# Gate taps of chunk 2 split over three engines in the last eight blocks, and a longer first loop

## The chip, the core and the metric

The kernel runs on one core of a Trainium2 chip. The metric is the device time of one launch in microseconds. A core has TensorE (PE, matrix products into PSUM), VectorE (DVE), ScalarE (ACT), GpSimd (POOL), and SyncE (SP), which here only issues DMAs. Each engine works through its own instructions in the order in which the program records them, and waits on semaphores for the others.

## The reference

A causal convolution over time with softmax weights per head, then a gated projection. For 8 sequences of 4224 tokens and 192 channels:

```python
w = exp(weight - weight.max(-1)); w = w / (w.sum(-1) + 1e-9)      # 8 heads, 7 taps
x2 = einsum('hk,bskhg->bshg', w, x_unf)                           # 7-tap causal convolution
gate_pre = sum(conv_w[k] * xp[:, k:k+S, :] for k in range(5))     # 5-tap causal convolution per channel
gate = 1 / (1 + exp(-gate_pre))
out = (gate * (x2 @ w_val)) @ w_out                               # 192 x 192 each
```

`xp` is the first convolution's output with four zero rows ahead of it.

## The kernel before, in words

**Layout.** The eight sequences are two streams of four sequences each, laid end to end. The 192 channels are split in two chunks. Chunk 1 is 128 channels on 128 partitions, with the two streams side by side (tile x1, so a block of m tokens is 128 x 2m). Chunk 2 is the other 64 channels, with the two streams stacked on 128 partitions (tile x2, a block is 128 x m). The tokens are cut into 14 groups, and these into 36 blocks, numbered 0 to 35: blocks 0 and 1 of about 303 tokens, 2 to 7 of 448, 8 to 31 of 502, 32 and 33 of 448, 34 of 500 and 35 of 188.

**The first convolution.** It is done by PE in units of four windows (`conv_unit`, L312), against a banded matrix. ACT copies each unit from PSUM to a tile e (L321), and DMAs from SP's queue spread the rows of e into x1 and x2 of a group (L350). A table `todo` says how many units are recorded in which block's pass: 3 in passes 0, 2, 6 and 7, five in passes 3 and 4, four in pass 5, 3, 3 and 4 in turn in the middle, 2 in passes 26 to 31, and none after.

**One block n.** The steps are functions that the loops call with a block's number.

- *The gate* is five taps per chunk. `gate_open(n, i)` (L384) is the first tap: ACT multiplies x by a column of weights into PSUM (pa for chunk 1, i = 0; pb for chunk 2, i = 1; one bank set each, so pa is opened for the next block only after it is closed). `gate_taps` (L391) is the other four: DVE instructions of the form x * weight + acc, in place in PSUM. `gate_close` (L404) is ACT's sigmoid into a tile g (g1 for chunk 1, g2 for chunk 2).
- *The split* (`split`, L412 and L420 on ACT, L413 and L421 on POOL): ACT rounds x to a short float xh, POOL subtracts to get the rest xl. The products with w_val are then made as wh xh + wl xh + wh xl.
- *The value product* v = x w_val is in three PSUM banks: bank 2 (`diagonal`, L447, then `columns`, L485) and banks 0 and 1 (`main`, L457, then `rows`, L470).
- `gated` (L504): DVE multiplies a bank of v by g in place. This is the last reader of that bank, so it also sets it free.
- `split_gated1` and `split_gated2`: the same split on g, ACT's ph and POOL's pl.
- *The output product* o = g w_out: the same four steps with ph and pl, one block later. `project` (L520) copies o to SBUF by ACT and issues the output DMA.

**Banks.** One pool of five PSUM banks ("p") serves v, o and the convolution units. A new tile takes the bank that was set free longest ago. The second bank of o in `rows("o", n-1)` takes the one that v's bank 2 of the same pass had, so it waits for `gated(n, 2)`.

**The order around the change.** The scheduler is off (`manual_schedule`): each engine runs what the two loops at the end record, in that order. A pass n of a loop makes v for block n, o for block n-1, and the gate of block n+1, and opens the gates of block n+2. The two loops differ in where DVE's and ACT's work stands. The first loop (passes 0 to HEAD-1, with HEAD = 4) records two chunk-1 taps of block n+1 ahead of `gated(n, ...)`, and the other two and the four chunk-2 taps behind it, and ACT closes pa of block n+1 late, among the convolution copies. The second loop (from pass HEAD on) records all four chunk-1 taps ahead of `gated(n, 2)`, closes and opens pa right after them, and records the four chunk-2 taps behind `gated(n, 1)`. `split(n+1)` stands in the front part of both.

Of the kernel before, what the change touches and what calls it, by code (L numbers as in the profile page):

```python
# [7 lines left out]
F32 = mybir.dt.float32  # L8
# [4 lines left out]
ALU = mybir.AluOpType  # L13
# [29 lines left out]
def second(n):  # L43
    return NS * n * WIN - reach(n)
# [24 lines left out]
STEPS = []  # L69
# [5 lines left out]
N = len(STEPS)  # L75
LAST = N - 1
MB = 502
# [24 lines left out]
def kernel(  # L102
# [9 lines left out]
    nc = tc.nc  # L112
# [6 lines left out]
    pp = ctx.enter_context(tc.tile_pool(name="pp", bufs=2))  # L119
    op = ctx.enter_context(tc.tile_pool(name="op", bufs=3))  # L120
# [54 lines left out]
    def scratch(n, i):  # L175
        o = scr_at[i]
        scr_at[i] += n
        return scr[i][:, o : o + n].bitcast(I32)

    raw = {}  # L180
    for name, ap, n, i in (("wv", wv, 2 * D + 2 * KG, 2), ("wo", wo, 2 * D, 1)):
        t = scratch(2 * n, i)
# [74 lines left out]
    cwt = cp.tile([128, 2, KG], F32, name="cwt")  # L257
# [107 lines left out]
    def views(n, k=KG - 1):  # L365
        g, o, m = STEPS[n]
        b = second(NJS[g])
        x1v = x1s[g][:, : 2 * b].rearrange("p (a t) -> p a t", a=2)
        return x1v[:, :, o + k : o + k + m], x2s[g][:, o + k : o + k + m]
# [5 lines left out]
    def gate_open(n, i):  # L375
        if n >= N:
            return
        m = STEPS[n][2]
        if i == 0:
            acc = ps_g.tile([128, 2, 512], F32, tag="pa", name=f"pa_{n}")[:, :, :m]  # L380
        else:
            acc = ps_h.tile([128, 512], F32, tag="pb", name=f"pb_{n}")[:, :m]
        accs[n, i] = acc
        nc.scalar.mul(acc, views(n, 0)[i], cwt[:, i, 0:1])  # L384

    def gate_taps(n, i, k0=1, k1=KG):
        if n >= N:
            return
        acc = accs[n, i]
        for k in range(k0, k1):  # L390
            nc.vector.scalar_tensor_tensor(  # L391
                out=acc, in0=views(n, k)[i], scalar=cwt[:, i, k : k + 1],
                in1=acc, op0=ALU.mult, op1=ALU.add,
            )

    def gate_close(n, i):
        if n >= N:
            return
        m = STEPS[n][2]
        if i == 0:  # L400
            dst = g1s[n] = gp.tile([128, 2, MB], F32, tag="g1", name=f"g1_{n}")[:, :, :m]
        else:
            dst = g2s[n] = gp.tile([128, MB], F32, tag="g2", name=f"g2_{n}")[:, :m]
        nc.scalar.activation(dst, accs.pop((n, i)), AF.Sigmoid)  # L404
# [3 lines left out]
    def split1(pool, tag, n, x):  # L408
        m = STEPS[n][2]
        h = pool.tile([128, 2, MB], F32R, tag="h", name=f"{tag}h_{n}")[:, :, :m]  # L410
        l = pool.tile([128, 2, MB], F32R, tag="l", name=f"{tag}l_{n}")[:, :, :m]
        nc.scalar.copy(h, x)  # L412
        nc.gpsimd.tensor_tensor(out=l, in0=x, in1=h.bitcast(F32), op=ALU.subtract)  # L413
        return h, l

    def split2(pool, tag, n, x):
        m = STEPS[n][2]
        h = pool.tile([128, MB], F32R, tag="h2", name=f"{tag}h2_{n}")[:, :m]
        l = pool.tile([128, MB], F32R, tag="l2", name=f"{tag}l2_{n}")[:, :m]
        nc.scalar.copy(h, x)  # L420
        nc.gpsimd.tensor_tensor(out=l, in0=x, in1=h.bitcast(F32), op=ALU.subtract)  # L421
        return h, l
# [3 lines left out]
    def bank(what, n, q):  # L426
        t = ps.tile([128, 512], F32, tag="p", name=f"{what}_{n}_{q}")[:, : STEPS[n][2]]
        banks[what, n, q] = t
        return t

    def operands(what, n):
        return (w_val, *xs[n, 1], *xs[n, 2]) if what == "v" else (w_out, *pr[n, 1], *pr[n, 2])

    def parts(w, h, l):
        return (w.h, h), (w.l, h), (w.h, l)

    def ok(n):
        return 0 <= n < N

    def diagonal(what, n):  # L440
        if not ok(n):
            return
        acc = bank(what, n, 2)
        w, _, _, h2, l2 = operands(what, n)
        r = slice(W22, W22 + 128)
        for i, (a, b) in enumerate(parts(w, h2, l2)):
            nc.tensor.matmul(acc, lhsT=a[:, r], rhs=b, start=(i == 0), stop=False)  # L447

    def main(what, n, q):
        if not ok(n):  # L450
            return
        fresh = (what, n, q) not in banks
        acc = bank(what, n, q) if fresh else banks[what, n, q]
        w, h, l, _, _ = operands(what, n)
        r = slice(W11, W11 + 128)
        for i, (a, b) in enumerate(parts(w, h, l)):
            nc.tensor.matmul(  # L457
                acc, lhsT=a[:, r], rhs=b[:, q], start=(fresh and i == 0), stop=(not fresh and i == 2)
            )

    def rows(what, n):
        if not ok(n):
            return
        fresh = (what, n, 0) not in banks
        two = [bank(what, n, q) if fresh else banks[what, n, q] for q in range(2)]
        w, _, _, h2, l2 = operands(what, n)
        r = slice(W21, W21 + 128)
        for i, (a, b) in enumerate(parts(w, h2, l2)):
            for acc, p in zip(two, HALVES):
                nc.tensor.matmul(  # L470
                    acc, lhsT=a[p, r], rhs=b[p], start=(fresh and i == 0), stop=(not fresh and i == 2)
                )

    def columns(what, n):
        if not ok(n):
            return
        m = STEPS[n][2]
        acc = banks[what, n, 2]
        w = w_val if what == "v" else w_out
        x = views(n)[0] if what == "v" else g1s[n]  # L480
        cuts = [m * i // 4 for i in range(5)]
        for i in range(4):
            c = slice(cuts[i], cuts[i + 1])
            for q, p in enumerate(HALVES):
                nc.tensor.matmul(  # L485
                    acc[p, c], lhsT=w.f[:, W12 : W12 + 64], rhs=x[:, q, c],
                    start=False, stop=(i == 3),
                )

    def split(n):  # L490
        if n >= N:
            return
        x1, x2 = views(n)
        if n == 0:
            xs[n, 2] = split2(sp, "x", n, x2)
        xs[n, 1] = split1(sp, "x", n, x1)
        if n > 0:
            xs[n, 2] = split2(sp, "x", n, x2)

    def gated(n, q):  # L500
        if not ok(n):
            return
        v = g1s[n][:, q] if q < 2 else g2s[n]
        nc.vector.tensor_tensor(out=v, in0=banks.pop(("v", n, q)), in1=v, op=ALU.mult)  # L504

    def split_gated1(n):
        if ok(n):
            pr[n, 1] = split1(pp, "p", n, g1s[n])

    def split_gated2(n):  # L510
        if ok(n):
            pr[n, 2] = split2(pp, "p", n, g2s[n])

    def project(n, q):
        if not ok(n):
            return
        m = STEPS[n][2]
        if n not in ots:
            ots[n] = op.tile([128, 3 * MB], F32, tag="ot", name=f"ot_{n}")
        nc.scalar.copy(ots[n][:, q * m : (q + 1) * m], banks.pop(("o", n, q)))  # L520
        o = 3 * sum(s[2] for s in STEPS[:n])
        if n == LAST:
            nc.sync.dma_start(out[:, o + q * m : o + (q + 1) * m], ots[n][:, q * m : (q + 1) * m])
        elif q == 1:
            nc.sync.dma_start(out[:, o : o + 3 * m], ots[n][:, : 3 * m])
# [34 lines left out]
    split(0)  # L560
    w_out.join(nc.gpsimd)
    gate_taps(0, 0)
    conv(first_unit[LAG] - done[0])
    gate_close(0, 0)
    gate_open(1, 0)
    w_out.cast(nc.gpsimd)
    gate_taps(0, 1)
    gate_close(0, 1)
    gate_open(1, 1)

    for n in range(HEAD):
        k = 2 if n < 2 else 3
# [150 lines left out]
```

## Time and profile before

| | |
|---|---|
| median of 3 runs | 390.23 us (390.02 to 390.97) |
| the profiled execution's own time | 393.35 us |
| its span in the profile | 391.6 us |
| granted TensorE clock, mean | 0.991 |
| busy share: PE, DVE, ACT, POOL | 97%, 87%, 83%, 65% |
| HBM traffic over the span | 141 GB/s |

Times in the profile's rows are microseconds from the span's start. A row of the timeline has a start, a time that it covers, the engine, the line of the code, the operation, output and inputs (buffer numbers left out), the shape and a count, and in brackets the engine's idle time ahead of it and what ended that. A row with a count above 1 is a run of equal instructions, and its second number covers the run. PE's matrix products are pipelined: the distance of two starts is what one takes from the engine. The profiled execution is 3.1 us longer than the median of the timed runs; differences are worked out against it.

### The profile page before, as it was taken

How to read it: one execution, taken by the hardware profiler on the slowest of the kernel's cores; microseconds unless marked ns; L12 is line 12 of the kernel's file. 1: busy time of each engine (PE TensorE's matmuls, PEld its weight loads, DVE VectorE, ACT ScalarE, POOL GpSimd, SP SyncE). 2: the span in 40 equal slices, each digit the busy share in tenths (PEclk: the TensorE clock that was granted, in tenths of full speed). 3: DMA queues.
4: the chain of work that ended last, by engine and by line, in shares of the span. 5: the costliest groups of instructions: out<-in, count | busy, mean ns of one | idle time of the engine just before them, and what ended most of it. 6: DMA issues, size and time to landing. Idle time of an engine off the chain costs nothing.

```text
span 391.6 us, 8620 instructions
## 1 busy us (share of the span) xinstructions
PE 378.0 (97%) x3204; PEld 321.6 (82%) x3204; DVE 342.3 (87%) x424; ACT 323.8 (83%) x525; POOL 254.8 (65%) x177
## 2 busy tenths in 40 slices
PE   8699999999999999999999999999999999999895
PEld 8687988898888888888888888888888787788684
DVE  4669899888998998998999899899899999999970
ACT  7458888988888888888889988888888888887863
POOL 1959765566667665666665666766566676776871
PEclk9969999999999999999999999999999999999999
DMA  8777869998687689778868868758987644333223
GB/s 293 210 195 223 253 214 290 258 239 272 210 251 216 180 260 256 210 217 253 224 194 256 219 185 261 218 178 253 257 226 227 211 160 146 114 135 133 80 106 144
DMA packets 38209, 82.49 MB, mean 211 GB/s; under 512 B 4856, under 2 KB 17528, under 8 KB 38168
## 3 DMA queue, kind: packets, MB, share of 16 engines
q1 hardware_dynamic: 36720, 79.90, 67.6%
q0 software_dynamic: 896, 1.31, 1.4%
q10 hardware_dynamic: 552, 0.73, 0.6%
q8 instruction: 25, 0.41, 0.5%
q14 instruction: 16, 0.13, 0.1%
HBM read 29.34 MB, written 26.00 MB: 141 GB/s over the span
## 4 chain that ended last, share of the span: by engine, by line
PE 72%; DVE 13%; DMA 5%; ACT 4%; issue 3%; SPq 2%; POOL 0%; DVEq 0%; ACTq 0%
PE pc L312 20%; PE o L457 10%; PE v L457 9%; PE v L485 7%; PE v L470 6%; PE o L485 6%; DVE pa L391 6%; PE o L470 5%; PE o L447 5%; PE v L447 4%; DVE pb L391 4%; DVE g L504 3%; DMA x<-e 2%; DMA x<-xw 2%; DMA scr<-wv 1%
## 5 line engine op out<-in xcount | busy, mean ns | idle before, releaser
L391 DVE SCALAR_TENSOR_TENSOR pa<-x,cwt,pa 128x1004 f32<-128x1004 f32 (+5 forms) x144 | 172.9, 1201 | 10.7 <-ACT pa L384 6.8
L413 POOL TENSOR_TENSOR xl<-x,xh 128x1004 fp32r<-128x1004 f32 (+5 forms) x36 | 74.8, 2077 | 73.1 <-ACT xh L412 58.9
L312 PEld LDWEIGHTS pc<-band,x 128*120 128x120 f32 x912 | 103.1, 187 | 7.1 <-issue 3.9
L312 PE MATMUL pc<-band,x 128*120 128x122 f32 x912 | 104.2, 272 | 4.3 <-DMA x<-xw 3.8
L391 DVE SCALAR_TENSOR_TENSOR pb<-x,cwt,pb 128x502 f32<-128x502 f32 (+5 forms) x144 | 102.2, 710 | 3.8
L413 POOL TENSOR_TENSOR pl<-g,ph 128x1004 fp32r<-128x1004 f32 (+5 forms) x36 | 79.4, 2204 | 10.3 <-ACT ph L412 7.7
L504 DVE TENSOR_TENSOR g<-v,g 128x502 f32<-128x502 f32 (+5 forms) x108 | 65.8, 642 | 21.1 <-PE v L470 16.1
L404 ACT ACTIVATE g<-pa 128x1004 f32<-128x1004 f32 (+5 forms) x36 | 34.5, 959 | 38.8 <-DVE pa L391 21.1
L321 ACT COPY e<-pc 120x488 f32<-120x488 f32 x114 | 59.1, 586 | 6.4 <-PE pc L312 6.3
L421 POOL TENSOR_TENSOR pl<-g,ph 128x502 fp32r<-128x502 f32 (+5 forms) x36 | 43.0, 1194 | 32.8 <-ACT ph L420 32.7
L520 ACT COPY ot<-o 128x502 f32<-128x502 f32 (+5 forms) x108 | 56.2, 551 | 3.3 <-PE o L457 2.6
L421 POOL TENSOR_TENSOR xl<-x,xh 128x502 fp32r<-128x502 f32 (+5 forms) x36 | 41.8, 1162 | 0.0
L384 ACT ACTIVATE pa<-x,cwt 128x1004 f32<-128x1004 f32 (+5 forms) x36 | 37.8, 1051 | 4.8 <-DMA x<-e 3.7
L485 PEld LDWEIGHTS v<-x,wvf 128*64 128x64 f32 x576 | 29.1, 136 | 11.8 <-issue 11.4
L485 PE MATMUL v<-x,wvf 128*64 128x125 f32 (+4 forms) x576 | 37.2, 270 | 0.0
L412 ACT CAST ph<-g 128x1004 fp32r<-128x1004 f32 (+5 forms) x36 | 35.1, 976 | 1.5 <-DVE g L504 1.5
L485 PE MATMUL o<-g,wof 128*64 128x125 f32 (+4 forms) x576 | 35.6, 264 | 0.0
L412 ACT CAST xh<-x 128x1004 fp32r<-128x1004 f32 (+5 forms) x36 | 34.6, 961 | 0.0
L485 PEld LDWEIGHTS o<-g,wof 128*64 128x64 f32 x576 | 30.9, 136 | 0.1
L457 PE MATMUL o<-ph,woh 128*128 128x502 f32 (+5 forms) x72 | 30.9, 429 | 0.0
L457 PE MATMUL v<-xh,wvh 128*128 128x502 f32 (+5 forms) x72 | 27.2, 377 | 0.3 <-ACT e L321 0.3
L457 PE MATMUL v<-xh,wvl 128*128 128x502 f32 (+5 forms) x72 | 27.1, 377 | 0.0
(75 smaller groups left out, 573.1 us busy)
## 6 DMA issues: line engine op xcount, KB each, us to landing
x<-xw SPq DMA_DIRECT2D x64, 300.0 KB
out<-ot SPq DMA_DIRECT2D x24, 753.0 KB
x<-e SPq DMA_DIRECT2D x40, 285.9 KB
x<-xw SPq DMA_DIRECT2D x20, 360.0 KB
out<-ot SPq DMA_DIRECT2D x8, 672.0 KB
x<-e SPq DMA_DIRECT2D x32, 141.6 KB
x<-e SPq DMA_DIRECT2D x25, 171.6 KB
x<-e SPq DMA_DIRECT2D x16, 94.4 KB
```

The costliest lines, as they stand in the source:

```text
L312: nc.tensor.matmul(pc[:M, k * WIN : (k + 1) * WIN], lhsT=xtiles[i][:, c : c + M], rhs=band[:, 4 * q + hi, :], start=True, stop=True,)
L321: nc.scalar.copy(e[:, a : a + w], pc[:M, :w])
L384: nc.scalar.mul(acc, views(n, 0)[i], cwt[:, i, 0:1])
L391: nc.vector.scalar_tensor_tensor(out=acc, in0=views(n, k)[i], scalar=cwt[:, i, k : k + 1], in1=acc, op0=ALU.mult, op1=ALU.add,)
L412: nc.scalar.copy(h, x)
L413: nc.gpsimd.tensor_tensor(out=l, in0=x, in1=h.bitcast(F32), op=ALU.subtract)
L421: nc.gpsimd.tensor_tensor(out=l, in0=x, in1=h.bitcast(F32), op=ALU.subtract)
L457: nc.tensor.matmul(acc, lhsT=a[:, r], rhs=b[:, q], start=(fresh and i == 0), stop=(not fresh and i == 2))
L470: nc.tensor.matmul(acc, lhsT=a[p, r], rhs=b[p], start=(fresh and i == 0), stop=(not fresh and i == 2))
L485: nc.tensor.matmul(acc[p, c], lhsT=w.f[:, W12 : W12 + 64], rhs=x[:, q, c], start=False, stop=(i == 3),)
L504: nc.vector.tensor_tensor(out=v, in0=banks.pop(("v", n, q)), in1=v, op=ALU.mult)
L520: nc.scalar.copy(ots[n][:, q * m : (q + 1) * m], banks.pop(("o", n, q)))
```

## The change

Two edits.

1. HEAD is 6 instead of 4, so that passes 4 and 5 run in the first loop's order.
2. A new step, `aside(n)`, for the blocks 28 to 35, recorded in the second loop behind `split(n+1)`. ACT multiplies the view of tap 3 of chunk 2 by its weight into a new tile t. The view of tap 4 is multiplied into a new tile u, by POOL for blocks 28 to 32, and by ACT for blocks 33 to 35. POOL adds u to t. For these blocks `gate_taps` does only taps 1 and 2 of chunk 2, and then DVE adds t to the accumulator pb.

```diff
-HEAD = 4
+HEAD = 6
+ASIDE, BOTH = 28, 33
...
+    asides = {}
+
+    def aside(n):
+        if not ASIDE <= n < N:
+            return
+        m = STEPS[n][2]
+        t = asides[n] = pp.tile([128, MB], F32, tag="t", name=f"t_{n}")[:, :m]
+        u = pp.tile([128, MB], F32, tag="u", name=f"u_{n}")[:, :m]
+        nc.scalar.mul(t, views(n, 3)[1], cwt[:, 1, 3:4])
+        if n < BOTH:
+            nc.gpsimd.tensor_scalar(
+                out=u, in0=views(n, 4)[1], scalar1=cwt[:, 1, 4:5], scalar2=None, op0=ALU.mult
+            )
+        else:
+            nc.scalar.mul(u, views(n, 4)[1], cwt[:, 1, 4:5])
+        nc.gpsimd.tensor_tensor(out=t, in0=t, in1=u, op=ALU.add)
...
     def gate_taps(n, i, k0=1, k1=KG):
...
+        if i == 1 and n in asides:
+            k1 = 3
         for k in range(k0, k1):
...
+        if i == 1 and n in asides:
+            nc.vector.tensor_tensor(out=acc, in0=asides.pop(n), in1=acc, op=ALU.add)
...
         split(n + 1)
+        aside(n + 1)
         diagonal("o", n - 1)
```

What it moves, engine by engine. VectorE in passes 4 to 6, before; pa and pb are the gate accumulators with the block's number behind them, g2 and g1 the outputs of `gated`:

```order
L391 SCALAR_TENSOR_TENSOR pa_5_819<-x1_2_387,cwt_155,pa_5_819 128x2x448 x4
L504 TENSOR_TENSOR g2_4_854<-v_4_2_858,g2_4_854 128x448
L504 TENSOR_TENSOR g1_4_817<-v_4_0_876,g1_4_817 128x448
L504 TENSOR_TENSOR g1_4_817<-v_4_1_880,g1_4_817 128x448
L391 SCALAR_TENSOR_TENSOR pb_5_856<-x2_2_388,cwt_155,pb_5_856 128x448 x4
L391 SCALAR_TENSOR_TENSOR pa_6_897<-x1_3_555,cwt_155,pa_6_897 128x2x448 x4
L504 TENSOR_TENSOR g2_5_989<-v_5_2_993,g2_5_989 128x448
L504 TENSOR_TENSOR g1_5_895<-v_5_0_1011,g1_5_895 128x448
L504 TENSOR_TENSOR g1_5_895<-v_5_1_1015,g1_5_895 128x448
L391 SCALAR_TENSOR_TENSOR pb_6_991<-x2_3_556,cwt_155,pb_6_991 128x448 x4
L391 SCALAR_TENSOR_TENSOR pa_7_1032<-x1_3_555,cwt_155,pa_7_1032 128x2x448 x4
L504 TENSOR_TENSOR g2_6_1122<-v_6_2_1126,g2_6_1122 128x448
```

The same engine from pass 5's first taps on in the changed kernel (its line numbers are 22 to 24 higher):

```order
L413 SCALAR_TENSOR_TENSOR pa_6_956<-x1_3_555,cwt_155,pa_6_956 128x2x448 x2
L528 TENSOR_TENSOR g2_5_989<-v_5_2_993,g2_5_989 128x448
L528 TENSOR_TENSOR g1_5_954<-v_5_0_1009,g1_5_954 128x448
L528 TENSOR_TENSOR g1_5_954<-v_5_1_1013,g1_5_954 128x448
L413 SCALAR_TENSOR_TENSOR pa_6_956<-x1_3_555,cwt_155,pa_6_956 128x2x448 x2
L413 SCALAR_TENSOR_TENSOR pb_6_991<-x2_3_556,cwt_155,pb_6_991 128x448 x4
L413 SCALAR_TENSOR_TENSOR pa_7_1094<-x1_3_555,cwt_155,pa_7_1094 128x2x448 x4
L528 TENSOR_TENSOR g2_6_1122<-v_6_2_1126,g2_6_1122 128x448
```

Two of the four chunk-1 taps have moved behind the three `gated` instructions in passes 4 and 5. The first pass with all four ahead of them is now pass 6.

GpSimd in pass 29 of the changed kernel; xl and xl2 are the rests of x for the next block, pl2 and pl those of g:

```order
L437 TENSOR_TENSOR xl_30_3924<-x1_11_3295,xh_30_3923 128x1004
L445 TENSOR_TENSOR xl2_30_3928<-x2_11_3296,xh2_30_3927 128x502
L399 TENSOR_SCALAR u_30_3932<-x2_11_3296,cwt_155 128x502
L404 TENSOR_TENSOR t_30_3931<-t_30_3931,u_30_3932 128x502
L445 TENSOR_TENSOR pl2_29_3972<-g2_29_3913,ph2_29_3971 128x502
L437 TENSOR_TENSOR pl_29_3994<-g1_29_3848,ph_29_3993 128x1004
```

Two instructions have come in between xl2 and pl2; before, these four stood one behind the other without them. VectorE at the end of pass 28 and in pass 29 of the changed kernel:

```order
L413 SCALAR_TENSOR_TENSOR pb_29_3804<-x2_11_3296,cwt_155,pb_29_3804 128x502 x2
L418 TENSOR_TENSOR pb_29_3804<-t_29_3820,pb_29_3804 128x502
L413 SCALAR_TENSOR_TENSOR pa_30_3850<-x1_11_3295,cwt_155,pa_30_3850 128x2x502 x4
L528 TENSOR_TENSOR g2_29_3913<-v_29_2_3917,g2_29_3913 128x502
L528 TENSOR_TENSOR g1_29_3848<-v_29_0_3940,g1_29_3848 128x502
L528 TENSOR_TENSOR g1_29_3848<-v_29_1_3944,g1_29_3848 128x502
```

Where four pb taps stood in a row, two are left, and the add that reads t stands between them and the next block's pa taps.

## The prediction

> **What bounds the kernel now.** I read the page first (PE is busy for 97% of the span, DVE for 87%), then the busy times by windows, then the timelines of PE, VectorE (DVE), ScalarE (ACT) and GpSimd (POOL) at three places: passes 3 to 7, passes 27 to 31, and pass 34. "Pass n" is the run of the loop for block n, and Tn is where its first product starts (L447, v from xh and wvh). A window late in the kernel (PE, PE's weight loads, DVE, ACT, POOL, then PE's granted clock and the DMA share):
>
> ```profile
> 331.00:341.00 10.00, 10.00 (x80) 8.03 (x82) 9.77 (x12) 8.74 (x14) 6.84 (x5) 1.00 0.33 112
> ```
>
> PE is full, and its clock is granted in full. But a PE that counts as busy can be one that is held, and DVE is full as well here (9.77 of 10). How much PE is held shows in the length of its passes, so I measure everything by these. Early, with the PE rows that open passes 4 to 8, the convolution units of passes 3 and 5, and the one product that waits:
>
> ```profile
> 58.85 4.36 PE L312 MATMUL pc<-band,x 128*120 128x122 f32 x40
> 62.98 0.45 PE L447 MATMUL v<-xh,wvh 128*128 128x448 f32 x1
> 68.97 0.47 PE L470 MATMUL o<-ph,woh 64*128 64x448 f32 x1 [0.59 <-DVE g L504]
> 75.24 0.45 PE L447 MATMUL v<-xh,wvh 128*128 128x448 f32 x1
> 82.30 3.52 PE L312 MATMUL pc<-band,x 128*120 128x122 f32 x32
> 85.58 0.45 PE L447 MATMUL v<-xh,wvh 128*128 128x448 f32 x1
> 95.08 0.45 PE L447 MATMUL v<-xh,wvh 128*128 128x448 f32 x1
> 105.06 0.47 PE L447 MATMUL v<-xh,wvh 128*128 128x502 f32 x1
> ```
>
> One unit costs 4.36 - 3.52 = 0.84 us. Pass 6, with three units, lasts 9.50; pass 5, with four, 10.34, just one unit more. So neither is held. Pass 4 with five should last 11.18 and lasts 12.26: it loses 1.08, at the product that waits for `gated` to free v's bank 2. Pass 7, three units, lasts 9.98 and loses 0.48.
>
> **Edit 1: the first order in passes 4 and 5.** DVE and ACT there:
>
> ```profile
> 62.62 1.01 ACT L384 ACTIVATE pa<-x,cwt 128x896 f32<-128x896 f32 x1
> ...
> 60.40 2.86 DVE L391 SCALAR_TENSOR_TENSOR pb<-x,cwt,pb 128x448 f32<-128x448 f32 x4
> 63.66 4.73 DVE L391 SCALAR_TENSOR_TENSOR pa<-x,cwt,pa 128x896 f32<-128x896 f32 x4 [0.41 <-ACT pa L384]
> 68.30 1.68 DVE L504 TENSOR_TENSOR g<-v,g 128x448 f32<-128x448 f32 x3
> 78.99 0.63 DVE L504 TENSOR_TENSOR g<-v,g 128x448 f32<-128x448 f32 x1 [1.60 <-PE v L485]
> 80.55 1.16 DVE L504 TENSOR_TENSOR g<-v,g 128x448 f32<-128x448 f32 x2 [0.93 <-PE v L470]
> ```
>
> Before, pass 4 has `gated` at 68.30, T4 + 5.32, and loses 1.08; so a 448-token pass loses what `gated` starts later than T + 4.24. With two taps ahead of it instead of four (4.64 us, so 2.32 less) DVE is ready at T4 + 3.0 and waits for PE's columns, T + 3.75 as in pass 5. **Pass 4 loses nothing: -1.08.**
>
> The work put off comes back in pass 6, the first of the second loop. In pass 5 the two chunk-1 `gated` start at T5 + 5.31 and end near 6.4; then come two pa taps (2.32) and four pb taps (2.8): DVE is through at T5 + 11.5, and pass 5 is 10.34, so T6 + 1.1. ACT is later still. In pass 3, which has the first order, pa is open at 62.62 + 1.01, which is 4.78 after the units begin at 58.85. In pass 5 they begin at T5 + 7.06, so pa of block 7 opens at T5 + 11.84, T6 + 1.50. Four taps of 4.64 from T6 + 1.53 put `gated(6, 2)` at T6 + 6.17, 1.93 past the limit. **Pass 6 loses 1.93.** Pass 7 then starts at T6 + 11.43; DVE is done with block 6 and the pb taps at T6 + 6.17 + 1.6 + 2.8 = T6 + 10.6, and its pa taps (5.08, from 315.12 to 320.20 below) end at T7 + 4.25: **the 0.48 of pass 7 goes.** Sum: -1.08 + 1.93 - 0.48 = **+0.37**. If ACT opens pa in time, DVE alone sets T6 + 1.1 and the sum is -0.06; if pass 7 keeps its 0.48 it is +0.85. Behind it PE stays the bound up to pass 25, so this is carried to the end. SP's and POOL's queues keep their order here.
>
> **Edit 2: prices.** Per block DVE loses two taps of 0.745 (from 312.14 to 315.12 for four, below) and gains one add:
>
> ```profile
> L504 DVE TENSOR_TENSOR g<-v,g 128x502 f32<-128x502 f32 x72 | 46.5, 676 | 12.1 <-PE v L470 11.4 <-PE v L485 0.4
> L413 POOL TENSOR_TENSOR xl<-x,xh 128x1004 fp32r<-128x1004 f32 x24 | 51.6, 2150 | 53.6 <-ACT xh L412 45.5 <-DMA x<-e 4.3 <-issue 2.2
> L421 POOL TENSOR_TENSOR xl<-x,xh 128x502 fp32r<-128x502 f32 x24 | 29.1, 1211 | 0.0
> L269 POOL MEMSET wof<- 128x128 f32 x1 | 0.2, 206 | 0.0
> L701 POOL MEMSET const-float32-1.0<- 128x1 f32 x1 | 0.1, 99 | 0.0
> ```
>
> The add reads PSUM and SBUF as `gated` does: 676 ns, 0.63 from start to start. So DVE saves 0.86 a block if it does not wait. POOL's add of t is the 1.21 row. POOL's multiply u is nowhere in the trace. Its upper end is the two-operand row, 1.21. Its lower end is a memset, which reads nothing: (206 - 99)/127 = 0.84 ns an element, 0.52 us for 502. Two operands cost (2150 - 1211)/502 = 1.87 ns an element; one operand less at half of that gives 1.21 - 0.47 = 0.74, which I take, between the ends and nearer to the write-only one. The Trainium skill, GPSIMD Engine Reference, section 3.1, gives 1.8 cycles an element at 1.2 GHz for the best one-input loop of that length and about 2.6 for two inputs; by that u would be an estimated 0.75 us, and the sum would be the same.
>
> ACT's multiply by a weight (0.6 to 0.7 us, as its casts) falls in the gap in which ACT waits for DVE's pa taps, 1.19 in the row below, so it costs nothing; if that gap closes, it is 0.6 a block.
>
> **Edit 2: passes 28 to 31.** PE's passes, DVE, ACT and POOL:
>
> ```profile
> 315.07 0.47 PE L447 MATMUL v<-xh,wvh 128*128 128x502 f32 x1
> 324.89 0.47 PE L447 MATMUL v<-xh,wvh 128*128 128x502 f32 x1
> 334.85 0.47 PE L447 MATMUL v<-xh,wvh 128*128 128x502 f32 x1
> 344.67 0.48 PE L447 MATMUL v<-xh,wvh 128*128 128x502 f32 x1
> 354.18 0.45 PE L447 MATMUL v<-xh,wvh 128*128 128x448 f32 x1
> ...
> 312.14 3.08 DVE L391 SCALAR_TENSOR_TENSOR pb<-x,cwt,pb 128x502 f32<-128x502 f32 x4
> 315.12 5.17 DVE L391 SCALAR_TENSOR_TENSOR pa<-x,cwt,pa 128x1004 f32<-128x1004 f32 x4
> 320.20 1.97 DVE L504 TENSOR_TENSOR g<-v,g 128x502 f32<-128x502 f32 x3
> 350.54 1.27 DVE L504 TENSOR_TENSOR g<-v,g 128x502 f32<-128x502 f32 x2 [0.38 <-PE v L470]
> ...
> 320.41 1.01 ACT L404 ACTIVATE g<-pa 128x1004 f32<-128x1004 f32 x1 [1.19 <-DVE pa L391]
> ...
> 308.49 2.15 POOL L413 TENSOR_TENSOR xl<-x,xh 128x1004 fp32r<-128x1004 f32 x1 [1.69 <-ACT xh L412]
> 310.60 1.26 POOL L421 TENSOR_TENSOR xl<-x,xh 128x502 fp32r<-128x502 f32 x1
> 318.84 2.15 POOL L413 TENSOR_TENSOR xl<-x,xh 128x1004 fp32r<-128x1004 f32 x1 [1.68 <-DMA out<-ot]
> 324.63 2.36 POOL L413 TENSOR_TENSOR pl<-g,ph 128x1004 fp32r<-128x1004 f32 x1 [0.21 <-ACT ph L412]
> 328.68 2.16 POOL L413 TENSOR_TENSOR xl<-x,xh 128x1004 fp32r<-128x1004 f32 x1 [1.69 <-ACT xh L412]
> ```
>
> Pass 31 lasts 9.51 and is not held; passes 28, 29 and 30 last 9.82, 9.96 and 9.82. Pass 28 has `gated` at T + 5.13 and loses 0.31, so here the limit is T + 4.82. All there is to gain is 0.31 + 0.45 + 0.31 = 1.07.
>
> The new wait: DVE's add needs t, and behind the add stand the next block's pa taps and `gated`. From xl's start t takes 2.11 + 1.26 + 0.74 + 0.2 (an instruction that waits) + 1.21, with 0.07 to DVE: 5.59.
> Pass 27: t arrives at 308.49 + 5.59 = 314.08, DVE would be there at 313.64; the pa taps start at 314.71 instead of 315.12. Pass 28: `gated` at 319.79, T + 4.72, no loss, T29 = 324.58. Its xl (318.84) was released ahead of any saving, so t is there at 324.43, while DVE is there at 323.7 (chunk 1's `gated` starts T + 5.87, as at 350.54); pa taps 325.06. Pass 29: `gated` at 330.14, T + 5.56, loses 0.74; T30 = 334.83. Its xl follows ACT's closing of pa (320.41) by 8.27, now 0.41 earlier: 328.27, t at 333.86, pa taps at 334.49. Pass 30: `gated` at T + 4.74, no loss, T31 = 344.34; t at 344.20, pa taps 344.83, `gated` T + 5.13. Pass 31 loses 0.31, T32 = 354.16 against 354.18. **Nothing is left: 0.0.** With u = 0.52 the same steps end 0.6 earlier, with 1.21 0.7 later.
>
> **Edit 2: the tail.** In pass 34 POOL's pl2 of block 33 now stands behind the add for block 34:
>
> ```profile
> 361.20 1.10 ACT L384 ACTIVATE pa<-x,cwt 128x1000 f32<-128x1000 f32 x1 [0.95 <-DMA x<-e]
> ...
> 369.25 0.47 PE L470 MATMUL o<-ph,woh 64*128 64x448 f32 x1 [0.78 <-DVE g L504]
> 372.49 0.36 PE L447 MATMUL o<-pl,woh 128*128 128x448 f32 x1
> ...
> 369.58 1.29 POOL L421 TENSOR_TENSOR xl<-x,xh 128x500 fp32r<-128x500 f32 x1
> 370.96 1.16 POOL L421 TENSOR_TENSOR pl<-g,ph 128x448 fp32r<-128x448 f32 x1
> ```
>
> pl2 ends at 372.12 and PE takes it at 372.49: 0.37 to spare. The add puts it 1.21 later, so PE waits **0.84**. What DVE saves in pass 33 (PE's idle 0.78) does not help: POOL's chain there hangs on ACT's opening at 361.20, which waits for a DMA. PE has no other hold behind 372.49.
>
> **Sum.** 393.35 + 0.37 + 0.0 + 0.84 = 394.6 for the profiled execution; the same +1.2 on the median is 391.4. Its own ends: -0.06 - 0.6 + 0.84 gives 390.4, 0.85 + 0.7 + 0.84 gives 392.6. A measurement here tells about 0.3% (1.2 us) from no change, so the forecast lies at that edge.
>
> **Rivals.** *GpSimd becomes the bound*: u costs the two-operand price or more. The place is DVE's add in passes 27 to 31; 0.1 us of u moves T32 by 0.2, so it decides from about 1.0 up. At 1.21: 0.37 + 0.7 + 0.84 = +1.9, 392.1. For it: POOL's neighbours are all at that price. Against: they read two tensors. The same page of the Trainium skill keeps to the rule to leave elementwise work on DVE, which would speak for this rival.
> *Faster*: t comes in time everywhere, since ACT and POOL pull ahead over several passes. Then the 1.07 of passes 28 to 30 and pass 33's 0.78 are gained, pl2 is in time, and with edit 1 the sum is -1.07 - 0.78 + 0.37 = -1.5: 388.7. For it: DVE at 9.77 of 10. Against: ACT runs the 8.27 us to xl without a gap.
> *Nothing*: edit 1 at its low end, and the 0.84 eaten by most of the 1.07 gained ahead of it: -0.06 - 0.8 + 0.84 is 0, so 390.2. For it: the 0.37 that pl2 has to spare shows that the tail is near balance. Against: the DMA that ACT waits for at 361.20 comes no earlier than the last units of pass 31.
>
> **How the numbers follow.** Forecast 0.43 (about half of it over the edge), GpSimd the bound 0.22, nothing 0.20, faster 0.15. Faster by over 0.3%: 0.15. Within: 0.21 + 0.20 + 0.04 = 0.45. Slower: 0.22 + 0.18 = 0.40. The range takes the forecast's two ends and reaches up by 0.2 for u above 1.21 and down most of the way to the faster case: 389.2 to 392.8.
>
> **What would show it.** Right: pass 4 near 11.2 and pass 6 near 11.4; DVE's add idle on POOL's t in most of passes 27 to 31; a PE wait on pl of 0.8 in pass 34; T32 - T27 unchanged. Wrong: passes 28 to 31 near 9.5 each with no idle ahead of the add; pass 6 near 9.5; or u well off 0.74.

## The result and the profile after

The changed kernel takes 392.79 us (median of 7 runs, 391.58 to 394.35) against 390.21 of the kernel before (7 runs in the same rounds, 390.02 to 390.97). The ratio is 1.0063, 95% interval 1.0041 to 1.0084: slower, by about 2.5 us. Its profiled execution took 392.53 us, with a span of 390.7.

That span is shorter than the 391.6 of before, although the kernel is slower: the profiled execution of before began its first pass at 25.24 us, the one of after at 21.97, 3.27 earlier, and in neither had the change acted by then. So I compare the two traces from T3 on (51.19 before, 48.16 after), where the blocks' passes have settled.

These are the same PE rows as those shown of before, for passes 4 to 8, with the start of pass 9 added and the product that waits in pass 6:

```profile
59.96 0.45 PE L471 MATMUL v<-xh,wvh 128*128 128x448 f32 x1
71.15 0.45 PE L471 MATMUL v<-xh,wvh 128*128 128x448 f32 x1
81.51 0.45 PE L471 MATMUL v<-xh,wvh 128*128 128x448 f32 x1
88.34 0.47 PE L494 MATMUL o<-ph,woh 64*128 64x448 f32 x1 [1.19 <-DVE g L528]
92.92 0.45 PE L471 MATMUL v<-xh,wvh 128*128 128x448 f32 x1
102.43 0.48 PE L471 MATMUL v<-xh,wvh 128*128 128x502 f32 x1
113.53 0.48 PE L471 MATMUL v<-xh,wvh 128*128 128x502 f32 x1
```

Of before, the start of pass 9 and, for the tail, those of passes 33 to 35:

```profile
115.80 0.48 PE L447 MATMUL v<-xh,wvh 128*128 128x502 f32 x1
...
362.13 0.37 PE L447 MATMUL v<-xh,wvh 128*128 128x448 f32 x1
...
371.39 0.39 PE L447 MATMUL v<-xh,wvh 128*128 128x500 f32 x1
...
378.75 0.25 PE L447 MATMUL v<-xh,wvh 128*128 128x188 f32 x1
```

Pass 4 lasts 11.19 instead of 12.26, pass 6 11.41 instead of 9.50, pass 7 9.51 instead of 9.98, pass 8 11.10 instead of 10.74. From T9 to T27 the passes of the two kernels are equal to within 0.03 us each.

The late stage, first by the window that was shown of before (busy times of PE, PE's weight loads, DVE, ACT, POOL, then PE's granted clock and the DMA share), then PE's rows that open passes 28 to 32:

```profile
331.00:341.00 10.00, 10.00 (x80) 7.96 (x79) 8.91 (x12) 9.32 (x15) 9.22 (x7) 1.00 0.32 113
```

```profile
312.81 0.47 PE L471 MATMUL v<-xh,wvh 128*128 128x502 f32 x1
...
322.89 0.47 PE L471 MATMUL v<-xh,wvh 128*128 128x502 f32 x1
...
333.20 0.47 PE L471 MATMUL v<-xh,wvh 128*128 128x502 f32 x1
343.07 0.48 PE L471 MATMUL v<-xh,wvh 128*128 128x502 f32 x1
...
353.11 0.45 PE L471 MATMUL v<-xh,wvh 128*128 128x448 f32 x1
```

DVE has fallen from 9.77 to 8.91 of 10 and GpSimd has risen from 6.84 to 9.22. Passes 28 to 31 last 10.08, 10.31, 9.87 and 10.04 (before: 9.82, 9.96, 9.82, 9.51): a DVE with less work, and longer passes. The groups of the new instructions (busy time, mean ns of one, idle time ahead and what ended it) and the line of the waits from 300 to 355 us (total, times, longest):

```profile
L399 POOL TENSOR_SCALAR u<-x,cwt 128x502 f32<-128x502 f32 x4 | 6.2, 1560 | 0.0
L404 POOL TENSOR_TENSOR t<-t,u 128x502 f32<-128x502 f32 x4 | 5.0, 1252 | 0.3
L397 ACT ACTIVATE t<-x,cwt 128x502 f32<-128x502 f32 x4 | 2.8, 712 | 0.0
```

```profile
DVE pb L418 <- POOL t L404: 5.7, 5, 1.5
```

The multiply u on GpSimd, with one tensor operand, takes 1560 ns, longer than the two-operand instructions of that size there (group means of 1210 to 1260). DVE's add waits for t in each of the five passes, 5.7 us in all. One such pass on POOL and DVE:

```profile
316.56 2.15 POOL L437 TENSOR_TENSOR xl<-x,xh 128x1004 fp32r<-128x1004 f32 x1 [0.52 <-ACT xh L436]
318.67 1.27 POOL L445 TENSOR_TENSOR xl<-x,xh 128x502 fp32r<-128x502 f32 x1
319.90 1.56 POOL L399 TENSOR_SCALAR u<-x,cwt 128x502 f32<-128x502 f32 x1
321.55 1.25 POOL L404 TENSOR_TENSOR t<-t,u 128x502 f32<-128x502 f32 x1
...
319.97 1.52 DVE L413 SCALAR_TENSOR_TENSOR pb<-x,cwt,pb 128x502 f32<-128x502 f32 x2
322.83 0.69 DVE L418 TENSOR_TENSOR pb<-t,pb 128x502 f32<-128x502 f32 x1 [1.34 <-POOL t L404]
```

From xl to the add 6.27 us pass (322.83 - 316.56); DVE is through with its two taps at 321.49 and stands. Behind the add stand the next block's pa taps (from 323.43 on), and behind these `gated`, for which PE waits.

The tail, PE's rows with the two waits, then ACT and POOL:

```profile
360.73 0.37 PE L471 MATMUL v<-xh,wvh 128*128 128x448 f32 x1
...
367.39 0.47 PE L494 MATMUL o<-ph,woh 64*128 64x448 f32 x1 [0.38 <-DVE g L528]
369.52 0.38 PE L471 MATMUL v<-xh,wvh 128*128 128x500 f32 x1
371.72 0.47 PE L471 MATMUL o<-pl,woh 128*128 128x448 f32 x1 [0.96 <-POOL pl L445]
378.09 0.25 PE L471 MATMUL v<-xh,wvh 128*128 128x188 f32 x1
...
359.74 1.10 ACT L387 ACTIVATE pa<-x,cwt 128x1000 f32<-128x1000 f32 x1 [0.91 <-DMA x<-e]
...
368.09 1.26 POOL L445 TENSOR_TENSOR xl<-x,xh 128x500 fp32r<-128x500 f32 x1
369.31 1.27 POOL L404 TENSOR_TENSOR t<-t,u 128x500 f32<-128x500 f32 x1
370.54 1.12 POOL L445 TENSOR_TENSOR pl<-g,ph 128x448 fp32r<-128x448 f32 x1
```

GpSimd's pl for block 33 stands behind the add, and PE waits 0.96 for it. Pass 32 lasts 7.62 (7.95 before), pass 33 8.79 (9.26), pass 34 8.57 (7.36). From T35 to the end of the span it is 12.61 after (390.7 - 378.09) and 12.85 before.

### The profile page after: what moved, and what is told of

Read it like the earlier page. It is cut to its first block, busy times and chain, and to the rows that moved or that the text cites. A ratio compares the mean times of both kernels' runs of the same rounds, so it can differ in the third digit from the quotient of the medians.

```text
span 390.7 us, 8635 instructions
## 1 busy us (share of the span) xinstructions
PE 376.7 (96%) x3204; PEld 318.6 (82%) x3204; DVE 336.3 (86%) x416; ACT 329.8 (84%) x536; POOL 270.7 (69%) x190
## 4 chain that ended last, share of the span: by engine, by line
PE 70%; POOL 9%; ACT 7%; DMA 5%; issue 4%; DVE 4%; ACTq 1%; SPq 1%; DVEq 0%; POOLq 0%
PE pc L315 19%; PE o L481 10%; PE v L481 9%; PE v L509 7%; PE o L509 6%; PE v L494 6%; PE o L494 5%; PE o L471 4%; PE v L471 4%; DMA x<-xw 3%; DMA x<-e 2%; DVE pa L413 2%; POOL pl L437 2%; POOL u L399 2%; POOL xl L445 2%
## 5 line engine op out<-in xcount | busy, mean ns | idle before, releaser
L315 PEld LDWEIGHTS pc<-band,x 128*120 128x120 f32 x912 | 100.9, 184 | 6.1 <-issue 2.3
L315 PE MATMUL pc<-band,x 128*120 128x122 f32 x912 | 102.1, 268 | 3.0 <-DMA x<-xw 2.3
L413 DVE SCALAR_TENSOR_TENSOR pb<-x,cwt,pb 128x502 f32<-128x502 f32 (+4 forms) x128 | 91.2, 713 | 3.3
L481 PE MATMUL v<-xl,wvh 128*128 128x502 f32 (+5 forms) x72 | 27.1, 377 | 0.0
```

Of the source, the lines that this page charges most:

```text
L315: nc.tensor.matmul(pc[:M, k * WIN : (k + 1) * WIN], lhsT=xtiles[i][:, c : c + M], rhs=band[:, 4 * q + hi, :], start=True, stop=True,)
L413: nc.vector.scalar_tensor_tensor(out=acc, in0=views(n, k)[i], scalar=cwt[:, i, k : k + 1], in1=acc, op0=ALU.mult, op1=ALU.add,)
L481: nc.tensor.matmul(acc, lhsT=a[:, r], rhs=b[:, q], start=(fresh and i == 0), stop=(not fresh and i == 2))
```

## The experiments

The time ahead of pass 3 differs by up to 3.4 us between executions of kernels that do the same there (T3 lies from 47.77 to 51.19 in the traces of this case), which widens the intervals of the ratios, while a pass that no edit touches has the same length in all traces to a few hundredths. So each kernel is read by its pass lengths, which come from the starts of PE's first product of each pass, and the timed ratio stands beside them where there were rounds.

| kernel | T27 - T3 | T32 - T27 | 32 + 33 | 34 | T35 - T3 | ratio to before, 95% interval |
|---|---|---|---|---|---|---|
| before | 253.50 | 49.49 | 17.21 | 7.36 | 327.56 | 1 |
| after | 254.30 | 50.65 | 16.41 | 8.57 | 329.93 | 1.0063 [1.0041, 1.0084] |
| e1_head_alone | 254.25 | 49.46 | 17.22 | 7.35 | 328.28 | 1.0026 [1.0002, 1.0050] |
| e2_aside_alone | 253.52 | 50.64 | 16.42 | 8.51 | 329.09 | 1.0018 [0.9993, 1.0044] |
| e3_u_by_act | 253.49 | 48.42 | 16.75 | 8.79 | 327.45 | 0.9987 [0.9966, 1.0008] |
| e4_taps_out | 253.45 | 48.11 | 15.93 | 8.19 | 325.68 | 0.9943 [0.9919, 0.9967] |
| e5_early_t | 253.57 | 48.20 | 16.43 | 8.76 | 326.96 | not timed in rounds |
| e7_act_order | 253.78 | 49.48 | 17.20 | 7.35 | 327.81 | not timed in rounds |
| e8_act_no_tail | 253.57 | 48.44 | 16.80 | 7.56 | 326.37 | 0.9980 [0.9954, 1.0006] |
| e9_u_two_operands | 253.51 | 49.55 | 16.41 | 8.47 | 327.94 | 1.0026 [1.0005, 1.0047] |
| e10_early_two | 253.51 | 48.20 | 16.42 | 7.35 | 325.48 | 0.9938 [0.9914, 0.9962] |
| e11_early_two_now | 253.00 | 48.18 | 16.43 | 7.36 | 324.97 | 0.9933 [0.9910, 0.9955] |

The ratios are to runs of the kernel before on the same chip in the same rounds. e6_forms has its own readings, below.

**The two parts, each alone.**

e1, against the changed kernel:

```diff
-ASIDE, BOTH = 28, 33
+ASIDE, BOTH = 99, 33
```

> Only the first order held for six blocks; no products aside. Theory A (most of the change's loss is GpSimd's product u and the add behind it, in passes 27 to 31 and 34): this part costs 0.76 us, the sum of what passes 4, 6, 7 and 8 showed in the changed kernel (-1.07, +1.91, -0.47, +0.36 against the kernel before), so a ratio of 1.002; passes 27 to 34 have the lengths of the kernel before to within 0.1. Rival B (the two parts act on each other, the later start of the late blocks makes DVE meet t badly): pass 8 does not lengthen by itself, this part costs 0.4 or less. Rival C (most of the loss is this part): 2 us or more, 1.005.

e2, against the changed kernel:

```diff
-HEAD = 6
+HEAD = 4
```

> Only the products aside, in blocks 28 to 35; the first order holds for four blocks as before. Theory A: passes 3 to 26 as in the kernel before; passes 27 to 31 together 1.2 us longer, passes 32 and 33 0.8 shorter, pass 34 1.2 longer; in all +1.4 us, a ratio of 1.0035. Rival B (the parts act on each other): under 0.5 us. Rival C (most of the loss is the first order): within 0.3 of nothing.

Measured: e1 lengthens T27 - T3 by 0.75 and leaves passes 27 to 34 as they were; its pass 8 is 11.09. e2 leaves passes 3 to 26 as they were, adds 1.15 in passes 27 to 31, takes 0.79 from passes 32 and 33 and adds 1.15 in pass 34: +1.53 up to T35. Each part has in it, pass by pass, what the changed kernel shows, so they do not act on each other; B falls, and C too: by the passes the products aside are the larger part (1.53 of 2.3). The timed ratios agree in sum (0.26% and 0.18% against 0.63%, with intervals of 0.25% each) but are too wide to rank the two.

**Who multiplies u.** Against e2:

```diff
-ASIDE, BOTH = 28, 33
+ASIDE, BOTH = 28, 28
```

> The products aside alone (first order for four blocks), but u too is multiplied by ScalarE in all eight blocks; GpSimd only adds. Theory A (GpSimd's u of 1.56 us, in series ahead of the add, is what holds DVE): t comes about 1.5 us earlier in passes 27 to 31, DVE's add waits for it no more, passes 28 to 31 are 9.5 to 9.9 us each, the five passes together 0 to 0.9 shorter than before instead of 1.2 longer; the tail as it is with the products aside (+0.4), in all -0.5 to +0.4 us. Rival D (the hand-over by three engines costs, whoever multiplies: ScalarE's second product of 0.65 us delays its closing of pa and its casts as much as GpSimd's u did): passes 27 to 31 still 0.8 us or more longer, in all +1 to +1.5.

Measured: passes 28 to 31 last 9.44, 9.51, 9.49 and 9.66, T32 - T27 is 48.42, 1.07 less than before and 2.22 less than in e2. DVE's waits for t from 300 to 355 us:

```profile
DVE pb L418 <- POOL t L404: 0.7, 2, 0.5
```

So 5.7 us of waiting have become 0.7, and ScalarE's four more products of 703 ns cost passes 28 to 30 nothing that shows. Theory A holds, with a little more gained up to T32 than the 0.9 it allowed; D falls. But two products a block fill ScalarE: the profile lists no idle time of it from pass 28 on until its opening in pass 32, and pass 31 lasts 9.66, where 9.45 is reached with GpSimd's u begun earlier (e5, below). The tail costs more than in e2 (passes 32 to 34 together 0.97 over before), so that T35 - T3 is only 0.11 below before and the timed ratio does not exclude 1.

**DVE's relief without any wait.** Against e2:

```diff
-        if i == 1 and n in asides:
+        if i == 1 and n >= ASIDE:
             k1 = 3
...
-        aside(n + 1)
```

> The first order for four blocks, and in blocks 28 to 35 the two taps of chunk 2's gate are left out altogether (no products aside, no add; the gate of that chunk is computed from three taps, so the output is not the reference's). It prices DVE's relief without any wait: 1.5 us a block. Theory A (DVE is the second bound there, and its relief would be worth the time that passes 28 to 30 and 33 lose): passes 28 to 31 are 9.5 us each, PE's wait of 0.78 in pass 33 goes, in all -1.1 to -1.9 us, a ratio of 0.995 to 0.997. Rival E (PE alone sets the passes, DVE's relief is worth nothing): within 0.4 us of the kernel before.

Measured: passes 28 to 31 at 9.43 to 9.45, T35 - T3 1.88 below before, the ratio 0.9943. A holds: DVE is the second bound there, and its relief is worth about 2 us. Only pass 34 went against it: it grows from 7.36 to 8.19 with no add in GpSimd's queue, since the passes ahead came early and GpSimd's chain there did not. PE waits for its xl (0.49 from the product before, where 0.22 is usual) and for its pl:

```profile
366.04 0.39 PE L471 MATMUL v<-xh,wvl 128*128 128x500 f32 x1
366.53 0.49 PE L471 MATMUL v<-xl,wvh 128*128 128x500 f32 x1
...
367.64 0.47 PE L471 MATMUL o<-pl,woh 128*128 128x448 f32 x1 [0.20 <-POOL pl L445]
```

**When t is made.** Against e2, the products aside are issued one pass earlier:

```diff
         split(n + 1)
-        aside(n + 1)
...
         gate_open(n + 2, 1)
+        aside(n + 2)
```

> First order for four blocks; the products aside as in the change (u by GpSimd), but issued one pass earlier, at the end of the pass before the one whose DVE add takes t. Theory A1 (GpSimd's throughput: xl 2.11 + 1.26, pl 1.26 + 2.35, u 1.56 and the add 1.25 are 9.8 us a pass, more than PE's 9.43): an early start helps the first pass only, passes 28 to 31 still settle near 9.8 to 9.9 us, T32 - T27 49.3 to 49.9 against 49.5 before and 50.6 with t in its old place. Theory A2 (only lateness: t comes 0.8 to 1.5 us after DVE is ready): passes 28 to 31 are 9.45 to 9.55, T32 - T27 is 48.1 to 48.5 as with u by ScalarE.

Measured: passes 28 to 31 last 9.44, 9.51, 9.44 and 9.45, T32 - T27 is 48.20, and DVE's add waits for nothing. A2 holds for these four passes. POOL's products u there:

```profile
315.24 1.54 POOL L399 TENSOR_SCALAR u<-x,cwt 128x502 f32<-128x502 f32 x1
...
324.98 1.55 POOL L399 TENSOR_SCALAR u<-x,cwt 128x502 f32<-128x502 f32 x1
...
334.52 1.56 POOL L399 TENSOR_SCALAR u<-x,cwt 128x502 f32<-128x502 f32 x1
...
344.30 1.41 POOL L399 TENSOR_SCALAR u<-x,cwt 128x448 f32<-128x448 f32 x1
```

From one u to the next 9.74, 9.54 and 9.78 us pass, and GpSimd has no idle time in them. So the 9.8 that A1 counted for a pass is near what GpSimd takes, and it is more than PE's 9.45; but GpSimd lives on its early start. In pass 27 t is ready 4.07 us ahead of DVE's add (307.86 and 311.93), in pass 31 still 3.18 (346.93 and 350.11). Four passes do not show what becomes of this over many. Behind them the tail loses 0.62 (passes 32 to 34 last 25.19 against 24.57): in pass 34 PE waits 0.67 for GpSimd's xl, which now stands behind the add for block 34, and that add waited 1.30 for ScalarE's u. What held DVE in the change was that t came late, at the end of a chain that starts inside the pass.

**What makes u dear.** Against e2, u is made in another way in each of the blocks 28 to 31:

```diff
+            x, w = views(n, 4)[1], cwt[:, 1, 4:5]
+            if n == 28:
+                nc.gpsimd.tensor_tensor(out=u, in0=x, in1=w.to_broadcast([128, m]), op=ALU.mult)
+            elif n == 29:
+                nc.gpsimd.tensor_scalar(out=u, in0=x, scalar1=0.5, scalar2=None, op0=ALU.mult)
+            elif n == 30:
+                nc.gpsimd.tensor_copy(out=u, in_=x)
+            elif n == 31:
+                nc.gpsimd.memset(u, 0.5)
```

> First order for four blocks, products aside, but u is made in another way in each block: block 28 as a two-operand product of x and the weight read as a broadcast; block 29 with a constant in place of the weight; block 30 as a copy with no weight; block 31 as a memset that reads nothing; block 32 as in the change (in blocks 29 to 31 the gate's fifth tap is therefore not the reference's). It prices u at 128x502. Theory F1 (the per-partition weight, a pointer operand, makes the one-input product dear): with the constant and as a copy 0.75 to 1.0 us, two operands 1.2, with the weight 1.56. Theory F2 (a one-input product is dear on GpSimd, whatever the weight): with the constant also 1.5 to 1.6, two operands 1.2. Theory F3 (it is the sharing of the SBUF port with DVE's products at that place, not the form): all readings 1.4 or more, memset 0.5.

```profile
308.36 1.06 POOL L401 TENSOR_TENSOR u<-x,cwt 128x502 f32<-128x502 f32 x1
...
318.71 1.49 POOL L403 TENSOR_SCALAR u<-x 128x502 f32<-128x502 f32 x1
...
328.15 0.62 POOL L405 COPY u<-x 128x502 f32<-128x502 f32 x1
...
338.99 0.52 POOL L407 MEMSET u<- 128x502 f32 x1
```

F2 holds: the tensor-by-scalar instruction is dear on GpSimd with a constant too (1.49, one reading), so the pointer to the weight adds about 0.07. It is not the number of operands: the same product with the weight read as a broadcast tensor takes 1.06, less than the 1.2 that F2 gave it. And it is not the place, so F3 falls: e9, below, takes 1.02 to 1.04 for that form beside the same two DVE taps as the 1.56 of the changed kernel, and in e5 the tensor-by-scalar product takes 1.54 to 1.56 at another place, beside DVE's pa taps.

**ScalarE's opening in pass 5.** Against e1, one unit's copy less stands ahead of the closing of pa:

```diff
         now = todo[n] if n == 0 else todo[n] // 2
+        if n == 5:
+            now = 1
```

> The first order for six blocks, no products aside, and in pass 5 only one unit's copy instead of two stands ahead of ScalarE's closing of pa and opening of the next pa. Theory A (pass 6's loss of 1.91 is set by ScalarE, which opens pa of block 7 at T6 + 1.5; DVE would be there at T6 + 1.1): pa opens 0.4 to 0.6 earlier, pass 6 takes 11.0 us, 0.4 less than the 11.41 with two copies. Rival G (DVE's put-off taps set it, ScalarE's opening only seems to): pass 6 stays within 0.1 of 11.41.

```profile
81.40 1.01 ACT L387 ACTIVATE pa<-x,cwt 128x896 f32<-128x896 f32 x1
...
82.44 4.73 DVE L413 SCALAR_TENSOR_TENSOR pa<-x,cwt,pa 128x896 f32<-128x896 f32 x4
```

With T6 at 81.38 pa is open at T6 + 1.03, DVE takes it at T6 + 1.06 without a wait, and pass 6 lasts 10.95 instead of 11.41. A holds. DVE alone is the next bound, where the prediction had put it (T6 + 1.1).

**The tail.** Against e3, the products aside are in blocks 28 to 33 only:

```diff
-        if not ASIDE <= n < N:
+        if not ASIDE <= n < 34:
```

> First order for four blocks; t and u both by ScalarE, and only in blocks 28 to 33; blocks 34 and 35 keep all taps on DVE. Theory A (in the tail the add for block 34 stands ahead of GpSimd's pl of block 33; without it that pl comes 1.2 us earlier): passes 27 to 31 as with u by ScalarE, 1.07 us shorter than before; passes 32 to 34 together 0.2 to 0.5 shorter than before instead of 0.97 longer; in all -1.2 to -1.6 us, a ratio of 0.996 to 0.997: faster than both kernels. Rival H (the tail is paced by the transfer that ScalarE's opening waits for, so that what passes 27 to 31 gain is given back whether or not the add is there): passes 32 to 34 0.7 us or more longer than before, in all within 0.4 us of before.

Measured: T32 - T27 48.44; pass 34 is 7.56 instead of 8.79 in e3, and PE's wait for pl there, 1.17 in e3, is down to about 0.2 (pass 34 is 0.20 above the 7.36 of before). Passes 32 to 34 together are 24.36, 0.21 below before: at A's edge, against H's price. T35 - T3 is 1.19 below before; the timed ratio (0.9980) is less of a gain than A's 0.996 to 0.997 and does not exclude 1. H's transfer still has a part: ScalarE's opening that waits for it comes at T32 + 7.15 here and at T32 + 6.51 in e10, below, where passes 32 to 34 take 0.59 less.

**u as a two-operand product, in its old place.** Against e2, one instruction is replaced:

```diff
-            nc.gpsimd.tensor_scalar(
-                out=u, in0=views(n, 4)[1], scalar1=cwt[:, 1, 4:5], scalar2=None, op0=ALU.mult
+            nc.gpsimd.tensor_tensor(
+                out=u, in0=views(n, 4)[1], in1=cwt[:, 1, 4:5].to_broadcast([128, m]), op=ALU.mult
             )
```

> As the products aside alone (first order for four blocks, t in its place in the change), with one difference: GpSimd makes u as a two-operand product with the weight read as a broadcast, 1.06 us (start to start 1.14) instead of 1.56 (1.62). Theory A (the price of u is the step of the sum that failed; by the prediction's replay 0.1 us of u moves T32 by 0.2): T32 - T27 falls from 50.64 to 49.6 to 50.0 us (49.49 before); the tail as with the products aside; in all +0.4 to +0.9 us. Rival D (the length of u hardly counts, the hand-over does): T32 - T27 stays at 50.3 or more.

```profile
L399 POOL TENSOR_TENSOR u<-x,cwt 128x502 f32<-128x502 f32 x4 | 4.1, 1025 | 0.0
```

```profile
DVE pb L418 <- POOL t L404: 3.3, 5, 1.0
```

u is 0.53 shorter, T32 - T27 1.09: the prediction's slope of 0.2 us for each 0.1 of u. It ends at 49.55, just under the range that I gave (49.6 to 50.0). D falls. The timed ratios of e9 (1.0026) and e2 (1.0018) cannot be told apart, so the timing does not show this gain; the pass lengths do.

**A version that beats both kernels.** e10 is e5 with the two-operand u of e9 and the end of the products aside of e8; against e5, beside the instruction shown for e9:

```diff
-ASIDE, BOTH = 28, 33
+ASIDE, BOTH = 28, 34
...
-        if not ASIDE <= n < N:
+        if not ASIDE <= n < 34:
```

> A version that takes up what the runs showed: first order for four blocks, products aside in blocks 28 to 33 only, issued one pass earlier, u as the two-operand product on GpSimd. Theory A: passes 28 to 31 at 9.45 us, T32 - T27 48.2; no add for block 34 ahead of GpSimd's pl, and t of block 33 in time, so passes 32 to 34 together 23.7 to 24.4 against 24.57 before; in all -1.5 to -2.1 us, a ratio of 0.995 to 0.996. Rival H (the transfer that ScalarE's opening of pa waits for in pass 32 paces the tail): the gain of 1.3 up to T32 stands, but passes 32 to 34 give back 0.5 or more, in all -0.3 to -0.8.

e11, against e10:

```diff
         now = todo[n] if n == 0 else todo[n] // 2
+        if n == 3:
+            now = 1
```

> The version before with one more edit: in pass 3 only one unit's copy instead of two stands ahead of ScalarE's closing of pa and opening of the next (the same edit as was tried in pass 5). Theory A (ScalarE's late opening sets the loss in the pass after it here too): pass 4 takes 11.7 to 11.9 us instead of 12.26; passes 5 and 6 unchanged; in all 0.3 to 0.5 us below the version before. Rival G (pass 4's loss is DVE's own four put-off taps): pass 4 stays within 0.1 of 12.26.

Measured: e10 has passes 28 to 31 at 9.44 to 9.51, passes 32 to 34 together at 23.77, and is 2.08 below before at T35; 388.36 us against 390.92, ratio 0.9938, interval 0.9914 to 0.9962, a little better than the 0.995 to 0.996 expected. H falls: once t is early and no add lies ahead of pl, nothing is given back. Its three edits against e5 were not tried one by one. e11 has pass 4 at 11.77 instead of 12.24, which confirms ScalarE's opening there too; its ratio, 0.9933, cannot be told from e10's.

## Why the prediction was right in direction and wrong in a step

The forecast was 391.4, +1.2 us; it came out at +2.6 timed and +2.13 from T3 in the traces. 392.79 lies just under the upper end of the range, 392.8. The terms beside the traces (the 0.07 that they leave of the 2.13 is spread over passes 9 to 26):

| term | predicted | measured | how |
|---|---|---|---|
| pass 4 | -1.08 | -1.07 | 11.19 - 12.26 |
| pass 6 | +1.93 | +1.91 | 11.41 - 9.50 |
| pass 7 | -0.48 | -0.47 | 9.51 - 9.98 |
| pass 8 | 0 | +0.36 | 11.10 - 10.74 |
| passes 27 to 31 | 0.0 | +1.16 | 50.65 - 49.49 |
| passes 32 and 33 | 0 | -0.80 | 16.41 - 17.21 |
| pass 34 | +0.84 | +1.21 | 8.57 - 7.36 |
| behind T35 | 0 | -0.24 | 12.61 - 12.85 |

**Edit 1.** The reading of passes 4 and 6 was right to 0.02 us, with its cause. DVE and ACT at T6 = 81.51:

```profile
81.98 1.01 ACT L387 ACTIVATE pa<-x,cwt 128x896 f32<-128x896 f32 x1
...
83.03 4.73 DVE L413 SCALAR_TENSOR_TENSOR pa<-x,cwt,pa 128x896 f32<-128x896 f32 x4 [0.40 <-ACT pa L387]
87.67 1.68 DVE L528 TENSOR_TENSOR g<-v,g 128x448 f32<-128x448 f32 x3
...
98.23 1.16 DVE L528 TENSOR_TENSOR g<-v,g 128x448 f32<-128x448 f32 x2 [0.50 <-PE v L494]
99.30 3.08 DVE L413 SCALAR_TENSOR_TENSOR pb<-x,cwt,pb 128x502 f32<-128x502 f32 x4
...
107.37 2.01 DVE L528 TENSOR_TENSOR g<-v,g 128x502 f32<-128x502 f32 x3
```

pa is open at T6 + 1.48 (predicted + 1.50), `gated` starts at T6 + 6.16 (+ 6.17), and e7 shows that the opening sets it. Wrong was that behind pass 7 "PE stays the bound", so that the 0.48 of pass 7 would be gone for good. DVE's taps start at 99.30, T7 + 6.38, because they stand behind a `gated` that waits for PE; in the trace of before they start at T7 + 6.38 as well, and the `gated` of pass 8 comes at T7 + 14.45 in both. Of before:

```profile
101.46 3.08 DVE L391 SCALAR_TENSOR_TENSOR pb<-x,cwt,pb 128x502 f32<-128x502 f32 x4
...
109.53 0.67 DVE L504 TENSOR_TENSOR g<-v,g 128x502 f32<-128x502 f32 x1
```

PE reaches pass 8 0.47 earlier and waits there instead: 0.36 of the 0.47 is given back. I had not asked what is late next. So the part costs 0.75 (e1), near the upper end of what I gave (-0.06 to +0.85).

**The step that failed: the price of u.** The prediction took "one operand less at half of that gives 1.21 - 0.47 = 0.74", with 0.52 and 1.21 as ends. It is 1.56, outside both. The working assumed that the price goes by operands read; e6 shows that it goes by the kind of instruction: a copy, one operand in and one out, takes 0.62, near the 0.74, but a product with a scalar takes 1.49 to 1.56, more than the two-operand product (1.06). The Trainium skill, GPSIMD Engine Reference, section 4.1, has one-input work on GpSimd at roughly line rate. The copy, 0.62, does not speak against that; the tensor-by-scalar product, 1.49 to 1.56, does. The prediction also had an estimated 0.75 from the 1.8 cycles an element of the Trainium skill, GPSIMD Engine Reference, section 3.1; that the loop behind that figure is a one-input product is the prediction's own reading, and u takes twice as long.

With that price the mechanism is the rival's, *GpSimd becomes the bound*, at the place that it named (DVE's add in passes 27 to 31) and past the point from which it was to decide (about 1.0). Its price of +1.9 in all came from u = 1.21; the traces show +2.1. That this lies so near, and inside the range, is in part luck. By the prediction's own slope the 0.82 that u is longer is worth about 1.6, and with pass 8's 0.36 the sum would be 0.37 + 0.36 + 1.6 + 0.84 = 3.2, an estimated 393.4 and outside; passes 27 to 31, the tail and the time behind T35 came out lower than in this sum, together by 1.1. The slope of the replay held (e9), its level did not: it put T32 at about +0.4 for u near 1.03 and e9 shows +0.06, so the chain from xl to the add was somewhat shorter than I had made it (6.27 in pass 28, where 5.59 and the 0.82 that u is longer make 6.41). A second reading of that rival, that GpSimd's load as such holds PE, is not what happened in these passes: e5 has the same load and no loss up to T32.

**What there was to gain** was put too low. The prediction took pass 31, 9.51, for a pass that is not held; with DVE relieved it lasts 9.45, and T32 - T27 falls by 1.38 in e4, not by 1.07.

**ScalarE's product at no cost** was right for one a block (712 ns; in e10 passes 28 to 31 last 9.44 to 9.51). For two a block it was not quite: e3 is faster than e2, but pass 31 gives back 0.2.

**The tail.** That the add ahead of pl costs PE a wait in pass 34 was right: 0.96 in the trace, 0.84 predicted; it is gone in e10 and about 0.2 in e8. That the savings of pass 33 "do not help" holds for the sum, though not pass by pass. Passes 32 and 33 get 0.80 shorter, since DVE has less to do; GpSimd's chain does not come earlier by as much, so pass 34 waits for longer, and e4 shows the same without any add. Together passes 32 to 34 cost +0.41, not +0.84. The difference lies in ACT's opening, which hangs on a DMA: it came at T32 + 6.63 instead of T32 + 7.02. GpSimd's pl starts 10.80 behind that opening in the changed kernel, in e2 and in e9, so with the opening of before the tail would have cost an estimated 0.41 + 0.39 = 0.80. Why the transfer landed earlier was not tried: the opening lies at T32 + 6.53 to 6.63 in these three kernels and at T32 + 6.77 to 7.19 in before, e1 and e7, whose late passes are the same. The 0.24 behind T35 is not clear of scatter: that stretch takes 12.57 to 12.71 in the changed kernel, e2 and e9, and 12.65 to 12.85 in before, e1 and e7.

**Faster** had 0.15 on the ground that t might come in time everywhere. The gain that it named was there (e4: 1.9 us; e10: 2.1), and edits to how, when and for which blocks t is made reach it. The change went the other way because t was asked for in the pass in which it was begun.

## What to carry to other kernels

Work that is taken from a full engine pays only if its result is ready before that engine asks for it: here the same instructions lose 1.2 us when they are begun in the pass that needs them and win 1.3 when they are begun one pass before. An operation that the trace does not show is not bounded by its neighbours on that engine: here these gave 0.52 to 1.21, and it took 1.56, so it is to be priced in a run of its own or given a wider range. An engine that takes on work has to be read for what stands behind that work in its queue. When a wait is removed, follow the engine that ended it through the next pass: what it could not do earlier is waited for there.

## What was not expected of the hardware

On GpSimd, at 128x502 in f32 and in neighbouring passes of one kernel (e6), a memset took 0.52 us, a copy 0.62, a product of two tensors with one read as a broadcast 1.06, an add of two full tensors 1.26 to 1.28, and a product of one tensor with a constant 1.49. The product with a weight for each partition took 1.56 in the changed kernel. From the two sizes of u in the changed kernel, 1412 ns for 448 and 1560 for 502, it grows by an estimated 2.7 ns an element ((1560 - 1412)/54). And the time ahead of pass 3 differed by up to 3.4 us between executions, more than any edit here was worth, while untouched passes kept their lengths to a few hundredths of a microsecond.
